# Pooled q and k summed on 128 partitions, dummy products between the first transposes, and a list schedule for a full TensorE clock

## The chip, the cores and the metric

The kernel runs on one core of one Trainium2 chip. The metric is device time in microseconds (us) for one execution. TensorE (PE) does the matrix products and transposes, VectorE (DVE) sums and elementwise work, ScalarE (ACT) activations and copies, GpSimd (POOL) some elementwise work, and SyncE (SP) issues the transfers.

## The reference

What is computed is an attention followed by two expert layers, all in float32. The attention is the sum of two parts: a local one, in which each position sees only positions less than 4 away, and a pooled one, in which q, k and v are averaged over groups of 4 positions (576 positions become 144), attended, and repeated 4 times.

```python
batch, n_heads, seq, head_dim = 4, 8, 576, 64        # q and k have a spread of 0.8, v of 0.1
q_d = q.reshape(B, H, Sd, factor, D).mean(axis=3)    # Sd = 144, factor = 4; k_d and v_d likewise
out_d = sm_attn(q_d, k_d, v_d)                       # softmax(q_d k_d^T / 8) v_d
out_up = np.repeat(out_d, factor, axis=2)
out_local = softmax(where(abs(i - j) < 4, q k^T / 8, -1e9)) v
x = (out_up + out_local) as 2304 tokens of 512
h = x @ w_in;   x = (s * max(h, 0)**2 + b) @ w_out   # 512 to 2048 and back
h = x @ w2_in;  out = (h - tanh(h)) @ w2_out
```

## The kernel before

Tokens are worked through in eight units of 288, two to a batch, for the first expert layer, and then in five blocks of 256 or 512 for the second. Each weight is split into a high and a low part, so that three products at the full rate of TensorE stand for one float32 product (`w_split`, `l1`, `l2_1`). A unit needs 16 steps; a step is 12 products `ph` into the hidden layer (L775), two activations and a split of the result on ScalarE and VectorE (`ph`, `gh`, `gl`), and, two steps later, 12 products `acc` (L808).

**Batch 0, at the start.** Its attention is done with dense products on TensorE: tokens of q and k are loaded (`tok`, SP, L511), transposed (`tokT`, L552, 36 transposes in 12 pieces), and copied to `KT` by VectorE (L560) and to `QT` by ScalarE (L556). Then come banded scores `S` (L582, L584), exponentials `bs` (L590), transposes `PT` (L597), and products with v, `O` (L607). The pooled part of this batch has the names `Sd`, `PdT` and `up`. `ORDER` lists these as words; `word` issues one. The word `k00` is a piece of k, `q00` of q. `warm` issues dummy products of the identity (L893) into a bank that nobody reads: 14 ahead of the words, and one ahead of each word that begins with e, f, p or u. Meanwhile the weights arrive in 32 pieces of 512 KB, and ScalarE and VectorE split them (`wraw`, `wf`, `w`; L707 to L761). SyncE's queue holds all these loads in one order.

**Batches 1 to 3.** The local attention of units 2 to 7 is on VectorE (`local_items`: products `pD`, sums `s`, weighted sums `O`), with shares for GpSimd (`pP`) and ScalarE (`pA`). At its end a unit's result `O` is transposed (`xt`, L305), the pooled part `upT` is added (`xq`, L323), and the sum is split (`xh` on ScalarE, `xl` on VectorE); the unit's first product L775 needs both. The pooled part is `down_items`, for each batch four rounds, one for each pair of heads (2m, 2m+1). A round loads q, k and v of both heads as two halves of 72 groups (L351, 72 partitions by two halves by two heads by 256 numbers). VectorE sums each four positions of q and of k (`pp`, L362, two sums a round), GpSimd those of v. Four transposes `qkps` (L384) bring q and k to 128 partitions, ScalarE copies them (`qkT`, L388, L389); then scores `S` (L400), exponentials `E`, `norm`, transposes `PT` (L436), and four products `up` (L451). The two heads of a round write `up` to partitions 0 to 63 and 64 to 127 of one bank, and one copy (L453) brings it to `upT`.

**What sets the order.** The body writes the instructions down step by step, with priorities; `list_schedule` then runs through time with the durations that `cost` gives, picks for each engine the ready instruction of best priority, and so fixes each engine's order. Engines keep that order at run time. `COLD` says until which time TensorE is taken to run at half speed: 55000 ns.

Of the kernel before, what the change touches and what calls it, by code (L numbers as in the profile page):

```python
# [29 lines left out]
G = S // 4  # L30
# [53 lines left out]
def attention_moe_moe_kernel(ctx: ExitStack, tc, q, k, v, w_in, w_out, s_in, b_in, w2_in, w2_out, out):  # L84
# [256 lines left out]
    def down_items(b):  # L341
# [3 lines left out]
        def load(hq):  # L345
            for nm, a in (("q", q), ("k", k), ("v", v)):
                base = (b * H + 2 * hq) * S * D
                t = raw_p.tile([128, 2, 2, 4, D], F32, tag="raw", name="raw72")
                for hf in range(2):
                    src = bass.AP(a.tensor, base + hf * GH * 4 * D, [[4 * D, GH], [S * D, 2], [1, 4 * D]])  # L350
                    sp.dma_start(out=t[:GH, hf].rearrange("p h r d -> p h (r d)"), in_=src)  # L351
                st[nm, hq] = t

        def padd(hq, nm):
            t = st[nm, hq]
            t2 = late.tile([GH, 2, 2, D], F32, tag="pp_" + nm, name="pp2")
            if nm == "v":
# [3 lines left out]
            else:  # L361
                dve.tensor_reduce(out=t2.rearrange("p a h d -> p (a h) d").unsqueeze(3),  # L362
                                  in_=t[:GH].rearrange("p a h r d -> p (a h) d r"), axis=AX, op=ALU.add)
            st[nm + "p", hq] = t2

        def loads(hq):
            def f():
                load(hq)
            return f

        def pools(hq):
            def f():
                for nm in "qkv":
                    padd(hq, nm)
            return f

        def qkt(hq):
            def f():
                if hq == 0:
                    upT[b] = late2.tile([128, 4, G], F32, tag="upT", name="upT")  # L380
                p_ = ps_sd.tile([128, 2, G], F32, tag="sd", name="qkps")
                for n, nm in enumerate("qk"):
                    for hf in range(2):
                        pe.transpose(p_[:, n, GH * hf:GH * hf + GH],  # L384
                                     st[nm + "p", hq][:, hf].rearrange("p h d -> p (h d)"), ident[:GH, :GH])
                t = late.tile([128, 2, G], F32, tag="qkT", name="qkT")

                act.activation(out=t[:, 0], in_=p_[:, 0], func=AF.Copy, scale=1.0 / 128.0)  # L388
                act.copy(out=t[:, 1], in_=p_[:, 1])  # L389
                st["T", hq] = t  # L390
            return f

        def scores(hq):
            def f():
                t = st["T", hq]
# [49 lines left out]
        def pvm(hq):  # L445
            def f():
                p_ = ps_sd.tile([128, G], F32, tag="sd", name="up")
# [8 lines left out]
        it.append((0, loads(0)))  # L456
        it.append((0, pools(0)))
        it.append((0, qkt(0)))
        for hq in range(4):
            if hq < 3:  # L460
                it.append((0, loads(hq + 1)))
            it.append((0.8, scores(hq)))
            it.append((0.8, norm(hq)))

            if hq < 3:
                it.append((0, pools(hq + 1)))
                it.append((0, qkt(hq + 1)))
            else:
                it.append((0, lambda: None))
            it.append((0, ptr(hq)))  # L470
            it.append((0, pvm(hq)))
# [815 lines left out]
COLD = 55000.0  # L1287
STORE_LAG = 8000.0

# [189 lines left out]
def list_schedule(ins, dep, soft, aps):  # L1479
# [22 lines left out]
    while wake:  # L1502
# [43 lines left out]
        while todo:  # L1546
# [10 lines left out]
            else:  # L1557
                go = end + ENG[eng[m]]
# [49 lines left out]
```

## Time and profile before

| | us |
|---|---|
| median of 3 runs | 946.79 (946.19 to 947.15) |
| the profiled execution | 947.49 |
| its span, first to last instruction | 945.7 |
| TensorE busy | 918.5 (97%) |
| VectorE busy | 730.3 (77%) |
| ScalarE busy | 504.1 (53%) |
| GpSimd busy | 155.0 (16%) |

The profiled execution is 0.7 us above the median, and 1.8 us of it lie outside the span. A busy share is a mean over stages that have different limits: what an edit is worth must be read in its own stage. Busy time of TensorE counts a product as long whether the clock is full or half, so the granted clock is read beside it.

### The profile page before, as it was taken

How to read it: one execution, taken by the hardware profiler on the slowest of the kernel's cores; microseconds unless marked ns; L12 is line 12 of the kernel's file. 1: busy time of each engine (PE TensorE's matmuls, PEld its weight loads, DVE VectorE, ACT ScalarE, POOL GpSimd, SP SyncE). 2: the span in 40 equal slices, each digit the busy share in tenths (PEclk: the TensorE clock that was granted, in tenths of full speed). 3: DMA queues.
4: the chain of work that ended last, by engine and by line, in shares of the span. 5: the costliest groups of instructions: out<-in, count | busy, mean ns of one | idle time of the engine just before them, and what ended most of it. 6: DMA issues, size and time to landing. Idle time of an engine off the chain costs nothing.

```text
span 945.7 us, 15470 instructions
## 1 busy us (share of the span) xinstructions
PE 918.5 (97%) x5690; PEld 822.7 (87%) x5690; DVE 730.3 (77%) x1156; ACT 504.1 (53%) x1270; POOL 155.0 (16%) x128
## 2 busy tenths in 40 slices
PE   7999999978999999998999999999999999999998
PEld 6888999868999999998999998888888888888886
DVE  4667899899899999997969767996768728676621
ACT  4679654534756557465668665663435415343321
POOL 1544343341411413133100000000000000000000
PEclk7559999997999999999999999999999999999999
DMA  9990042423214231231129978764443744442061
GB/s 227 319 340 36 27 159 63 144 86 99 88 61 137 68 118 39 65 95 43 48 68 397 345 279 275 258 212 155 132 136 112 254 146 140 151 135 88 30 193 45
DMA packets 82354, 137.39 MB, mean 145 GB/s; under 512 B 23414, under 2 KB 49254, under 8 KB 82278
## 3 DMA queue, kind: packets, MB, share of 16 engines
q1 hardware_dynamic: 80662, 134.04, 43.3%
q10 hardware_dynamic: 1616, 2.36, 0.9%
q8 instruction: 45, 0.74, 0.3%
q14 instruction: 31, 0.25, 0.1%
HBM read 111.66 MB, written 24.71 MB: 144 GB/s over the span
## 4 chain that ended last, share of the span: by engine, by line
PE 77%; DVE 10%; ACT 8%; issue 3%; SPq 1%; DMA 1%; DVEq 0%; ACTq 0%
PE acc L1039 20%; PE ph L775 18%; PE wb L1178 16%; PE acc L808 14%; ACT pA L254 2%; PE S L584 2%; DVE s L195 2%; DVE xq L323 1%; DVE pD L190 1%; PE O L607 1%; DVE O L266 1%; SPq L511 1%; ACT E L410 1%; PE warm L893 1%; DVE gl L796 1%
## 5 line engine op out<-in xcount | busy, mean ns | idle before, releaser
L775 PE MATMUL ph<-xh,w 128*128 128x288 f32 x1024 | 235.6, 304 | 2.5 <-DVE gl L796 1.7
L808 PE MATMUL acc<-gh,w 128*128 128x288 f32 (+1 forms) x1024 | 227.7, 298 | 1.5 <-DVE yst L831 0.9
L775 PEld LDWEIGHTS ph<-xh,w 128*128 128x128 f32 x1024 | 174.3, 192 | 8.7 <-DVE gl L796 3.7
L808 PEld LDWEIGHTS acc<-gh,w 128*128 128x128 f32 x1024 | 171.4, 189 | 3.0 <-issue 1.7
L775 PE MATMUL ph<-xl,w 128*128 128x288 f32 x512 | 154.5, 302 | 0.2 <-DVE xl L327 0.2
L808 PE MATMUL acc<-gl,w 128*128 128x288 f32 x512 | 151.4, 296 | 0.7 <-DVE gl L796 0.7
L1178 PE MATMUL wb<-xoh,w1r 128*128 128x512 f32 x448 | 147.4, 393 | 0.0
L1039 PE MATMUL acc<-w2r,gx 128*128 128x512 f32 x576 | 137.2, 390 | 0.0
L1039 PEld LDWEIGHTS acc<-w2r,gx 128*128 128x128 f32 x576 | 108.1, 188 | 23.3
L787 ACT ACTIVATE ph<-ph 128x288 f32<-128x288 f32 x128 | 50.8, 398 | 105.6 <-PE ph L775 101.8
L1178 PEld LDWEIGHTS wb<-xoh,w1r 128*128 128x128 f32 x448 | 83.9, 187 | 20.1 <-ACT w1r L1111 0.2
L775 PEld LDWEIGHTS ph<-xl,w 128*128 128x128 f32 x512 | 98.2, 192 | 1.4 <-issue 0.6
L808 PEld LDWEIGHTS acc<-gl,w 128*128 128x128 f32 x512 | 96.7, 189 | 1.5 <-DVE gl L796 0.9
L1178 PE MATMUL wb<-xol,w1r 128*128 128x512 f32 x224 | 88.2, 394 | 0.0
L796 DVE TENSOR_TENSOR gl<-ph,gh 128x288 fp32r<-128x288 f32 x128 | 57.8, 452 | 29.9 <-ACT gh L793 28.9
L254 ACT ACTIVATE pA<-V,a 128x64 f32<-128x64 f32 x198 | 54.0, 341 | 9.8 <-DVE a L243 6.1
L1172 DVE TENSOR_TENSOR u<-wb,u 128x512 f32<-128x512 f32 x64 | 43.9, 686 | 16.2 <-PE wb L1178 16.2
L793 ACT CAST gh<-ph 128x288 fp32r<-128x288 f32 x128 | 50.7, 398 | 6.4 <-PE acc L808 3.1
L1164 DVE TENSOR_TENSOR gx<-gT,gx 128x512 fp32r<-128x512 f32 x32 | 22.0, 689 | 39.0 <-ACT gx L1163 39.0
L788 ACT ACTIVATE ph<-ph 128x288 f32<-128x288 f32 x128 | 50.8, 398 | 2.4
L1178 PEld LDWEIGHTS wb<-xol,w1r 128*128 128x128 f32 x224 | 42.0, 187 | 9.6
L362 DVE TENSOR_REDUCE pp<-raw 72x256 f32<-72x1024 f32 x24 | 48.6, 2028 | 0.4 <-DMA raw<-in_q_dram 0.4
(167 smaller groups left out, 1573.1 us busy)
## 6 DMA issues: line engine op xcount, KB each, us to landing
w2r<-keep_b SPq DMA_DIRECT2D x48, 512.0 KB
wraw<-in_moe_w_in_dram SPq DMA_DIRECT2D x32, 512.0 KB
wraw<-in_moe_w_out_dram SPq DMA_DIRECT2D x32, 512.0 KB
w1f<-keep_a SPq DMA_DIRECT2D x32, 256.0 KB
w1f<-keep_s SPq DMA_DIRECT2D x32, 256.0 KB
keep_b<-w SPq DMA_DIRECT2D x12, 512.0 KB
y<-yst SPq DMA_DIRECT2D x36, 144.0 KB
K<-in_k_dram SPq DMA_DIRECT2D x5, 960.0 KB
```

What stands on the lines that cost most here:

```text
L254: act.activation(out=p_[:, t, h], in_=Vt[u][:, h, o + t], func=AF.Copy, scale=st["a"][:, h * TAU + t, o:o + 1])
L362: dve.tensor_reduce(out=t2.rearrange("p a h d -> p (a h) d").unsqueeze(3), in_=t[:GH].rearrange("p a h r d -> p (a h) d r"), axis=AX, op=A ...
L775: pe.matmul(p_, w_, x_, start=n == 0, stop=n == 3 * KC - 1)
L787: act.activation(out=p_, in_=p_, func=AF.Relu)
L788: act.activation(out=p_, in_=p_, func=AF.Square)
L793: act.copy(out=gh[:, :NB1], in_=p_)
L796: dve.tensor_tensor(out=gl, in0=p_, in1=gh[:, :NB1].bitcast(F32), op=ALU.subtract)
L808: pe.matmul(accs[u][e][:, :g_.shape[1]], w_, g_, start=i == first and n == 0, stop=i == last and n == 2)
L1039: pe.matmul(accs[j][t], g_, x_, start=i == 0 and n == 0, stop=i == NF - 1 and n == 2)
L1164: dve.tensor_tensor(out=t[:, 1], in0=g_, in1=t[:, 0].bitcast(F32), op=ALU.subtract)
L1172: add = lambda o, x, y: dve.tensor_tensor(out=o, in0=x, in1=y, op=ALU.add)
L1178: pe.matmul(b_, w1_op(q_, o, kc, i), xo[x][m][:, kc], start=n == 0, stop=n == 5)
```

## The change

It has three parts.

1. In `down_items`, q and k of a batch are no longer loaded by pairs of heads. The 4 x 144 = 576 groups of heads 0 to 3 are cut into rows of 128 (`ROWS`: 128, 128, 128, 128, 64); one tile holds such a row block of q and k, for heads m and m+4 side by side. One VectorE sum works on q and k together, so that a batch has 5 sums where it had 8 (15 for 24 in three batches), and 10 transposes where it had 16. All of a batch's pooled q and k stand in one tile `qkT` of 576 columns, and a round takes heads (m, m+4). The products `up` of a round write both heads to the same 64 partitions, side by side in columns; the copy to `upT` has 64 partitions by 288 columns where it had 128 by 144. The v part is as before, in functions of its own. The order of the items changes with it.
2. `word` issues three dummy products ahead of each of the 12 words k and q: 36 products.
3. In `list_schedule`, TensorE is taken to be at half speed until 6000 ns, where it was 55000, and an instruction of TensorE that depends on VectorE or ScalarE is taken to be ready 300 ns later (`SLACK`).

```diff
+        ROWS = [min(128, 4 * G - 128 * n) for n in range(5)]
+        def load(n):
+            def f():
+                t = raw_p.tile([128, 2, 2, 4, D], F32, tag="raw", name="rawqk")
+                for x, a in enumerate((q, k)):
+                    src = bass.AP(a.tensor, b * H * S * D + 128 * n * 4 * D, [[4 * D, ROWS[n]], [4 * S * D, 2], [1, 4 * D]])
+                    sp.dma_start(out=t[:ROWS[n], x].rearrange("p h r d -> p h (r d)"), in_=src)
...
-                dve.tensor_reduce(out=t2.rearrange("p a h d -> p (a h) d").unsqueeze(3),
-                                  in_=t[:GH].rearrange("p a h r d -> p (a h) d r"), axis=AX, op=ALU.add)
+        def pools(n):
+            def f():
+                r = ROWS[n]
+                t2 = late.tile([128, 2, 2, D], F32, tag="pp_qk", name="ppqk")
+                dve.tensor_reduce(out=t2[:r].rearrange("p a h d -> p (a h) d").unsqueeze(3),
+                                  in_=st["raw", n][:r].rearrange("p a h r d -> p (a h) d r"), axis=AX, op=ALU.add)
...
+                for x in range(2):
+                    pe.transpose(p_[:, x, :r], st["pp", n][:r, x].rearrange("p h d -> p (h d)"), ident[:r, :r])
+                t = st["T"][:, :, 128 * n:128 * n + r]
...
-                for kh in range(2):
-                    for h in range(2):
-                        pe.matmul(p_[64 * h:64 * h + 64, :], vp[:, kh, h, :], st["PT", hq][h][:, kh, :],
-                                  start=kh == 0, stop=kh == 1)
-                act.copy(out=upT[b][:, hq, :], in_=p_)
+                r = slice(64 * (hq % 2), 64 * (hq % 2) + 64)
+                for h in range(2):
+                    for kh in range(2):
+                        pe.matmul(p_[r, h], vp[:, kh, h, :], st["PT", hq][h][:, kh, :], start=kh == 0, stop=kh == 1)
+                act.copy(out=upT[b][r, hq // 2::2, :], in_=p_[r])
...
+        for f in (load(0), load(1), pools(0), qkt(0), load_v(0), pools(1), qkt(1), pool_v(0), load(2)):
+            it.append((0, f))
+        for m in range(4):
+            it.append((0, scores(m)))
...
+        if c in "kq":
+            warm(3)
...
-COLD = 55000.0
+COLD = 6000.0
+SLACK = 300.0
...
+                if eng[m] == "PE" and e in ("DVE", "Activation"):
+                    go += SLACK
```

The third part moves instructions on every engine. Three places follow; rows of the changed kernel have line numbers 3 to 5 higher.

The first is TensorE's queue at the start. Before, 14 dummies, the 36 transposes `tokT`, and then scores `S` one group at a time, with transposes `PT` after the second:

```order
L893 MATMUL warm<-ident 128x128 x14
L552 MATMUL tokT<-ident,tok 128x128 x36
L582 MATMUL S<-bandr,identr 96x408
L584 MATMUL S<-KT,QT 96x102 x4
L582 MATMUL S<-bandr,identr 96x408
L584 MATMUL S<-KT,QT 96x102 x4
L597 MATMUL PT<-ident,bs 102x96 x4
```

Now 17 dummies stand first, then four transposes and three dummies in turn, later three and three; the end of that row and the scores behind it are:

```order
L896 MATMUL warm<-ident 128x128 x3
L555 MATMUL tokT<-ident,tok 128x128 x2
L896 MATMUL warm<-ident 128x128 x3
L555 MATMUL tokT<-ident,tok 128x128 x2
L585 MATMUL S<-bandr,identr 96x408 x4
L587 MATMUL S<-KT,QT 96x102 x16
L585 MATMUL S<-bandr,identr 96x408
L587 MATMUL S<-KT,QT 96x102 x2
L600 MATMUL PT<-ident,bs 102x96
L587 MATMUL S<-KT,QT 96x102
```

Four score groups now stand in a row, and the first `PT` follows in the sixth group's place, one transpose at a time. ScalarE's queue up to the first activation of `ph` holds 27 passes over raw weights, 9 weight casts and 6 copies `bPT` before, and 24, 6 and 7 now.

The second place is TensorE where the first product of unit 2 needs its tokens. Before, all products of the units ahead of it are done, and then come the nine transposes `xt`:

```order
L808 MATMUL acc<-gl,w 128x288
L808 MATMUL acc<-gh,w 128x288
L305 MATMUL xt<-ident,O 128x128 x9
L384 MATMUL qkps<-ident,pp_2710 128x72 x2
L384 MATMUL qkps<-ident,pp_2712 128x72 x2
L400 MATMUL S<-qkT 72x144 x2
L775 MATMUL ph<-xh,w 128x288 x2
```

Now:

```order
L457 MATMUL up<-PTs,pp_2430 64x144 x4
L305 MATMUL xt<-ident,O 128x128 x4
L811 MATMUL acc<-gh,w 128x288
L811 MATMUL acc<-gl,w 128x288
L811 MATMUL acc<-gh,w 128x288
L778 MATMUL ph<-xh,w 128x288
L305 MATMUL xt<-ident,O 128x128 x4
L778 MATMUL ph<-xl,w 128x288
L778 MATMUL ph<-xh,w 128x288
L811 MATMUL acc<-gh,w 128x288
```

The transposes moved ahead of some 45 products of the units before; the ninth stands in the middle of them, and unit 2's own products follow after all of them.

The third is VectorE where the pooled part of batch 1 begins. Before:

```order
L823 COPY yst<-acc 128x288
L362 TENSOR_REDUCE pp_1740<-raw_1731 72x256
L362 TENSOR_REDUCE pp_1742<-raw_1734 72x256
L796 TENSOR_TENSOR gl<-ph,gh 128x288 x2
L195 TENSOR_REDUCE s<-pD 128x18
L407 TENSOR_REDUCE nm<-S 72x2 x2
L195 TENSOR_REDUCE s<-pP 128x18
```

Now:

```order
L826 COPY yst<-acc 128x288
L195 TENSOR_REDUCE s<-pD 128x18
L379 TENSOR_REDUCE ppqk<-rawqk 128x256
L799 TENSOR_TENSOR gl<-ph,gh 128x288 x2
L195 TENSOR_REDUCE s<-pP 128x18
L379 TENSOR_REDUCE ppqk<-rawqk 128x256
L799 TENSOR_TENSOR gl<-ph,gh 128x288
```

The first round's scores wait for two sums in both. From the start of VectorE's queue to its first `xq` of unit 2 there are 10 pooled sums before (8 of batch 1, 2 of batch 2) and 6 now (5 and 1), and one sum `s`, one `gl` and two additions `yst` fewer.

## Rows read from the trace of the kernel before

**Rows 1.** The page, part 1 and part 2: TensorE's busy time, granted clock in 40 slices.

```profile
PE 918.5 (97%) x5690; PEld 822.7 (87%) x5690; DVE 730.3 (77%) x1156; ACT 504.1 (53%) x1270; POOL 155.0 (16%) x128
PEclk7559999997999999999999999999999999999999
```

**Rows 2.** Stretches: start:end and length, busy us by engine, granted clock, DMA share, GB/s.

```profile
9.40:12.80 3.40, 1.44 (x9) 0.93 (x9) 1.73 (x3) 0.92 (x2) 0.00 (x0) 1.00 1.30 230
17.80:70.40 52.60, 52.60 (x266) 44.13 (x265) 33.86 (x82) 36.43 (x98) 22.38 (x23) 0.50 1.01 319
70.80:97.00 26.20, 25.98 (x205) 23.43 (x205) 18.98 (x45) 25.52 (x71) 11.94 (x9) 1.00 0.09 35
120.00:205.70 85.70, 84.78 (x641) 79.29 (x639) 77.86 (x111) 44.07 (x142) 33.33 (x33) 1.00 0.37 115
205.70:210.60 4.90, 0.00 (x0) 0.01 (x1) 4.90 (x7) 1.15 (x2) 0.88 (x2) 1.00 0.25 38
210.60:220.40 9.80, 6.70 (x26) 4.74 (x27) 9.80 (x19) 3.88 (x12) 5.61 (x2) 0.51 0.58 202
220.40:224.40 4.00, 4.00 (x18) 4.00 (x19) 3.73 (x3) 1.98 (x7) 1.27 (x1) 0.50 0.22 74
224.40:500.00 275.60, 269.88 (x2072) 261.67 (x2072) 250.35 (x363) 163.85 (x537) 67.67 (x34) 0.99 0.25 79
```

**Rows 3.** Timeline of TensorE at the start: start us, length us, what, records, idle before.

```profile
1.45 5.53 PE L893 MATMUL warm<-ident 128*128 128x128 f32 x28 [1.45 <-POOL ident L117]
6.82 1.91 PE L552 MATMUL tokT<-ident,tok 128*128 128x128 f32 x16
...
13.72 2.58 PE L552 MATMUL tokT<-ident,tok 128*128 128x128 f32 x11 [0.81 <-DMA tok<-in_q_dram]
```

**Rows 4.** Timeline of ScalarE, and its groups of lines from 14 to 70.4 us.

```profile
17.78 0.67 ACT L707 ACTIVATE wraw<-wraw 128x512 f32<-128x512 f32 x1 [0.34 <-DMA wraw<-in_moe_w_in_dram]
70.42 0.41 ACT L787 ACTIVATE ph<-ph 128x288 f32<-128x288 f32 x1
...
L707 ACT ACTIVATE wraw<-wraw 128x512 f32<-128x512 f32 x18 | 12.1, 677 | 1.1 <-DMA wraw<-in_moe_w_in_dram 1.1
L758 ACT CAST w<-wf 128x512 fp32r<-128x512 f32 x9 | 5.6, 624 | 0.8 <-DVE wf L753 0.8
```

**Rows 5.** SyncE's queue: the transfers of the weight pieces 13 to 16.

```profile
34.78 3.66 SPq L694 DMA_DIRECT2D wraw<-in_moe_w_out_dram  x4
```

**Rows 6.** VectorE: pooled sums (page, part 5), and other instructions in the timeline.

```profile
L362 DVE TENSOR_REDUCE pp<-raw 72x256 f32<-72x1024 f32 x24 | 48.6, 2028 | 0.4 <-DMA raw<-in_q_dram 0.4
...
17.20 1.15 DVE L570 TENSOR_REDUCE qd<-QT 128x72 f32<-128x288 f32 x3
33.27 0.45 DVE L627 TENSOR_REDUCE bnm<-Sd 72x2 f32<-72x288 f32 x1 [1.24 <-PE Sd L623]
...
199.73 0.46 DVE L796 TENSOR_TENSOR gl<-ph,gh 128x288 fp32r<-128x288 f32 x1 [0.23 <-ACT gh L793]
...
205.88 1.34 DVE L195 TENSOR_REDUCE s<-pD 128x18 f32<-128x1152 f32 x1
207.14 0.81 DVE L826 TENSOR_TENSOR yst<-acc,yst 128x288 f32<-128x288 f32 x2
```

**Rows 7.** TensorE: products `up` and `S` of the pooled part, two records to a product.

```profile
153.25 0.46 PE L451 MATMUL up<-PTs,pp 72*64 72x144 f32 x2
155.29 0.71 PE L400 MATMUL S<-qkT 64*72 64x144 f32 x4
440.44 0.71 PE L451 MATMUL up<-PTs,pp 72*64 72x144 f32 x8
```

**Rows 8.** The copies to `upT`: min/median/max ns, first and last start us.

```profile
L453 ACT COPY upT<-up x12: 268/278/280, 155.4 to 441.2; 128x144 f32<-128x144 f32 x12
```

**Rows 9.** Waits: who waited for whom, us in total, times, longest.

```profile
PE xt L305 <- DVE O L266: 4.9, 1, 4.9
DVE nm L407 <- PE S L400: 2.0, 5, 0.6
```

More of the change, by code (lines that the diff above doesn't have):

```diff
@@ L343, in down_items, with load_v, pool_v, f @@
         st = {}
-        def load(hq):
-            for nm, a in (("q", q), ("k", k), ("v", v)):
-                base = (b * H + 2 * hq) * S * D
+        ROWS = [min(128, 4 * G - 128 * n) for n in range(5)]
[5 more added lines that the diff above has]
+                    sp.dma_start(out=t[:ROWS[n], x].rearrange("p h r d -> p h (r d)"), in_=src)
+                st["raw", n] = t
+            return f
+        def load_v(m):
+            def f():
                 t = raw_p.tile([128, 2, 2, 4, D], F32, tag="raw", name="raw72")
                 for hf in range(2):
-                    src = bass.AP(a.tensor, base + hf * GH * 4 * D, [[4 * D, GH], [S * D, 2], [1, 4 * D]])
+                    src = bass.AP(v.tensor, (b * H + m) * S * D + hf * GH * 4 * D, [[4 * D, GH], [4 * S * D, 2], [1, 4 * D]])
                     sp.dma_start(out=t[:GH, hf].rearrange("p h r d -> p h (r d)"), in_=src)
[L352 to L357, printed above, removed]
+                st["v", m] = t
+            return f
+        def pool_v(m):
+            def f():
+                t = st["v", m]
+                t2 = late.tile([GH, 2, 2, D], F32, tag="pp_v", name="pp2")
                 t1 = t[:GH, :, :, 0:2, :]
@@ L369, in loads, with qkt @@
             return f
-        def pools(hq):
+        def qkt(n):
             def f():
[L373 to L379, printed above, removed]
-                    upT[b] = late2.tile([128, 4, G], F32, tag="upT", name="upT")
[L381 to L390, printed above, removed]
+                if n == 0:
+                    upT[b] = late2.tile([128, 4, G], F32, tag="upT", name="upT")
+                    st["T"] = late.tile([128, 2, 4 * G], F32, tag="qkT", name="qkT")
+                r = ROWS[n]
+                p_ = ps_sd.tile([128, 2, 128], F32, tag="sd", name="qkps")
+                for x in range(2):
+                    pe.transpose(p_[:, x, :r], st["pp", n][:r, x].rearrange("p h d -> p (h d)"), ident[:r, :r])
+                t = st["T"][:, :, 128 * n:128 * n + r]
+                act.activation(out=t[:, 0], in_=p_[:, 0, :r], func=AF.Copy, scale=1.0 / 128.0)
+                act.copy(out=t[:, 1], in_=p_[:, 1, :r])
@@ L394, in f @@
             def f():
-                t = st["T", hq]
+                t = st["T"][:, :, G * hq:G * hq + G]
                 ps = []
@@ L446, in f @@
             def f():
-                p_ = ps_sd.tile([128, G], F32, tag="sd", name="up")
+                p_ = ps_sd.tile([128, 2, G], F32, tag="sd", name="up")
                 vp = st["vp", hq]
-                for kh in range(2):
-                    for h in range(2):
-                        pe.matmul(p_[64 * h:64 * h + 64, :], vp[:, kh, h, :], st["PT", hq][h][:, kh, :],
-                                  start=kh == 0, stop=kh == 1)
-                act.copy(out=upT[b][:, hq, :], in_=p_)
-            return f
[L456 to L471, printed above, removed]
+                r = slice(64 * (hq % 2), 64 * (hq % 2) + 64)
[3 more added lines that the diff above has]
+                act.copy(out=upT[b][r, hq // 2::2, :], in_=p_[r])
+            return f
+        for f in (load(0), load(1), pools(0), qkt(0), load_v(0), pools(1), qkt(1), pool_v(0), load(2)):
+            it.append((0, f))
+        for m in range(4):
+            it.append((0, scores(m)))
+            if m < 3:
+                it.append((0, load_v(m + 1)))
+            it.append((0, norm(m)))
+            if m < 3:
+                for f in (pools(m + 2), qkt(m + 2), pool_v(m + 1)):
+                    it.append((0, f))
+            if m < 2:
+                it.append((0, load(m + 3)))
+            it.append((0, ptr(m)))
+            it.append((0, pvm(m)))
         return it
```

7 lines of the change are left out of this document (3 added, 4 removed).

## The prediction

> **What bounds the kernel now.** First the page: TensorE is busy 918.5 of 945.7 us, so nearly every microsecond saved must come out of TensorE's row. But busy time at half clock counts double, and the row of the granted clock shows two weak slices after the first, up to about 71 us [rows 1]. So next come the stretches, each with its clock [rows 2]. Three kinds can be told apart.
>
> From 17.8 to 70.4 us TensorE is busy without a gap at a granted clock of 0.50, that is at 1.2 GHz of 2.4. ScalarE is busy 36.4 of the same 52.6 us, VectorE 33.9: TensorE bounds this stretch, and only because its clock is low. From 70.8 to 97 us ScalarE is full (25.5 of 26.2), with TensorE full beside it. From 120 to 224 us VectorE works almost without rest (77.9 of 85.7, then 4.9 of 4.9, 9.8 of 9.8): TensorE runs out of work at 205.7, stands still for 4.9 us, is fed badly to 220.4, and has half clock from about 210.8 to 224.4. The waits name the cause: `xt` for VectorE's `O` [rows 9]. After that TensorE loses 5.7 us in 276 [rows 2].
>
> Why does the clock fall at the start? From 9.4 to 12.8 us TensorE ran only nine transposes, 1.4 us of work, while it waited for tokens, and it has half clock from then on [rows 2, 3].
>
> **The dummies.** The price of one: a transpose of the same shape takes 1.91/16 = 0.12 us at full clock [rows 3], a dummy is two such records, so 0.24 us; the 14 first dummies took 5.53 us, 0.40 each, mostly before the clock had risen, and half of that is 0.20. I take 0.22; 36 cost 7.9 us. Where TensorE waited for tokens (9.4 to 13.7) they cost nothing. In all, from 6.8 us: 3 dummies, 36 transposes at 0.12, 33 dummies at 0.22 end near 19.1, where the transposes ended at 16.3 before. So the scores start some 3 us later. In return the clock should not fall at 12.8, since TensorE then has no idle time there: half of its work is products like those that raised the clock at first.
>
> **The start at full clock.** TensorE's 52.6 us become 26.3, so ScalarE is the bound. Its queue up to the first activation of `ph` now holds 3 raw-weight passes and 3 casts fewer and one copy more: 3 x 0.68 + 3 x 0.62 - 0.48 = 3.4 us less [rows 4]. Its second piece still lands at 17.8 [rows 4], as the transfers keep their order. So 33.0 us of work from 17.8: no earlier than 50.8. It idled 16.2 us; its waits go round by VectorE and TensorE, and the later scores keep 3 us of them. I take half, 8.1 us: first activation at 58.9 where it was at 70.4 [rows 4], 11.5 us earlier. The 3.4 us that were put off are paid in the stretch where ScalarE is full, which leaves **-8 us**. Bounds: no idle at all, -16; the clock falls again, 0 (a rival). Transfers forbid nothing here: the first activation stands behind 16 weight pieces, and those are issued by 38.4 us [rows 5].
>
> **The pooled sums.** A sum of 72 partitions by 1024 numbers takes 2.03 us [rows 6]. The row of before has none of this kind on 128 partitions. If time went by all elements it would be 2.03 x 128/72 = 3.61, and 15 of them 54 us against 48.6; but a sum of 288 numbers takes 0.45 on 72 partitions and 1.15/3 = 0.38 on 128 [rows 6], so I take 2.03: 9 fewer save 18.3 us of VectorE. What that is worth depends on the place. Ahead of unit 2's first `xq` VectorE has 4 pooled sums fewer (8.1), one `s` (1.34), one `gl` (0.46) and two `yst` (0.81) [rows 6]: 10.7 us. TensorE's loss there is 18.7 us (205.7 to 224.4) less its work, 10.7 at half clock or 5.35 at full: 13.3 us. VectorE's 10.7 are less than that; the transposes now stand ahead of some 45 products, which cover the addition and the split behind them. I take **-10 us**. Bounds: the 4.9 us wait alone, and all 13.3.
>
> From 224 to 500 us TensorE loses 5.7 us idle, and a mean clock of 0.99 is 0.01 x 275.6 = 2.8 us of full clock [rows 2]: 8.5. The other sums saved help here, but VectorE is 91% busy and each late piece has its own chain. I take about a third, **-3 us**, between 0 and -8.5.
>
> **The products `up`.** Here the change costs. One product takes 0.46 us from issue to end; four of them in the two partition halves take 0.71. Two score products of the same 144 columns in one half take 0.71 already [rows 7]. So products in different halves of the array run side by side, and a further one in the same half adds 0.71 - 0.46 = 0.25. Now all four of a round write one half: 0.46 + 3 x 0.25 = 1.21, 0.50 more, 12 times: **+6 us** on TensorE; 0 if they fall where it waits.
>
> **What I cost at nothing.** 30 transposes for 48, of 128 rows for 72, are about equal (the same 3 us). ScalarE has 30 copies `qkT` for 24, 6 x 0.28 us if these cost as much as the copies to `upT` [rows 8], and the 12 copies to `upT` have twice the columns, at most 12 x 0.28 more: 5 us in all, in stretches where it is busy under 60% [rows 2]; if that cover went, the scores would come later by these. SyncE issues 54 loads a run for 72, and as many bytes. A sum needs its one buffer `ppqk` free, so VectorE can wait for TensorE's transposes of the block before; two buffers of one entry had the same rule before, and no such wait is in the rows.
>
> **Sum.** Against the profiled execution: 947.5 - 8 - 10 - 3 + 6 = 932.5 us. That run lay 0.7 above the median: 931.8, say **932**. With every term at its good end it would be 909, with every one at its bad end and the clock held 947.5 - 0 - 4.9 - 0 + 6 - 0.7 = 948.
>
> **The rivals.**
>
> *The clock holds through the first transposes and falls again among the scores.* For it: from 17.8 to 70.4 TensorE was without a gap and the clock still did not rise [rows 2], so this mix, products of 64 rows and transposes, is weak; at full speed it would also have gaps. Against it: from 120 to 205.7 TensorE had 0.9 us of idle time and full clock throughout [rows 2], so short gaps alone don't lower it. Then TensorE stays the bound, its work begins 3 us later, and the start gains nothing: 947.5 - 10 - 3 + 6 - 0.7 = 940. The Trainium skill has a rule for this, "TensorE: Matmul & The Clock Gate", section "Part 4: PE-mode transpose": a transpose does not count as work in the way that a product does when the clock is decided. The trace agrees as far as it goes: the fall at 12.8 followed a stretch of transposes alone. By that rule the many `PT` and `PdT` behind the scores would not hold the clock, and the time would be this rival's.
>
> *The dummies don't do what they are for.* The clock falls at 12.8 all the same. The 21 dummies then left cost 0.40 to 0.47 each, and everything is later by 9 us at a TensorE that is the bound: 947.5 + 9 - 10 - 3 + 6 - 0.7 = 949. Against it: the idle time that preceded the fall is filled.
>
> *Unit 2 waits for something else.* VectorE is done in time, but its `O` also needs shares from ScalarE and GpSimd, and `upT` needs four rounds; then only some 3 of the 10 us come: 939.
>
> *The order costs more than it gives (slower).* The 300 ns make the schedule put TensorE's transposes and scores behind products of the steps, while VectorE or ScalarE waits for them. There are 75 such crossings in the pooled rounds (25 a batch) and 18 sets `xt`, 93 in all; with VectorE 91% busy a wait of it is not repaid. From 15/93 = 0.16 us more at each the change loses; at 0.25 us it is +23, 955. Against it: VectorE waited only 2.0 us in five times for `S` [rows 9].
>
> **How the numbers follow.** Forecast 0.53, clock falls later 0.20, unit 2 held by another 0.10, dummies fail 0.07, order 0.10. Leaving out the last two and a thin tail below, the range is 915 to 945. Faster by over 0.2% (less than that can't be told from no change) 0.83, within 0.2% 0.05, slower 0.12.
>
> **What would show it.** In the profile after: a granted clock of 1.00 from 12.8 to beyond 20 us; first activation of `ph` near 59; 15 sums at 2.0 us; no wait of 4.9 us for `O`, and clock 1.00 at the start of unit 2; four `up` at about 1.2 us. I am wrong if the sums grow with partitions, if the clock reads 0.50 in the score stretch, or if TensorE's idle time between 224 and 600 us grows.

## The result, and the profile after

The changed kernel takes **930.62 us** (median of 4 runs, 929.73 to 934.84) beside 946.72 for the kernel before in the same series: a ratio of 0.9834, with a 95% interval from 0.9812 to 0.9855, so 16 us faster. The profiled execution has a span of 929.0 us, where it was 945.7.

The page's part 1 and its row of the granted clock, in 40 slices, to be read beside [rows 1]:

```profile
PE 909.0 (98%) x5744; PEld 814.6 (88%) x5744; DVE 705.8 (76%) x1147; ACT 506.0 (54%) x1276; POOL 151.9 (16%) x128
PEclk9869999999999999999999999999999999999999
```

TensorE is busy 9.5 us less although it runs 36 dummies more (and 18 transposes fewer; two records to each). The stretches of the changed kernel (start:end and length, busy us of PE, PEld, DVE, ACT and POOL with their counts, granted clock, DMA share, GB/s) answer to [rows 2]:

```profile
12.80:40.40 27.60, 27.26 (x245) 23.30 (x243) 18.75 (x52) 20.39 (x64) 9.06 (x9) 1.00 1.06 276
40.40:61.00 20.60, 17.22 (x93) 14.20 (x93) 15.16 (x36) 16.84 (x39) 7.67 (x9) 0.50 0.97 309
17.80:60.05 42.25, 38.54 (x285) 31.56 (x285) 29.58 (x81) 33.09 (x94) 16.37 (x17) 0.77 1.02 285
70.80:97.00 26.20, 26.20 (x215) 24.07 (x216) 17.73 (x46) 25.46 (x72) 9.14 (x7) 1.00 0.14 57
186.70:198.40 11.70, 10.90 (x83) 9.93 (x81) 11.70 (x22) 5.26 (x14) 4.46 (x2) 1.00 0.42 134
198.40:224.00 25.60, 24.64 (x180) 23.25 (x180) 25.20 (x36) 16.36 (x52) 8.28 (x3) 1.00 0.48 150
224.00:500.00 276.00, 271.10 (x2031) 261.16 (x2032) 238.42 (x373) 170.44 (x539) 69.63 (x32) 1.00 0.29 96
```

The clock is full from 12.8 to 40.4 us, falls to half until about 61, and is full to the end. The row from 17.80 ends at the first activation of `ph`; it will be read against the prediction's sum for the start. Unit 2 starts at 198.4 us without the idle 4.9 us before it and at a full clock. The new sums (VectorE's groups of lines, by form: busy us and mean ns) and a round of `up` (TensorE's timeline: start, length) answer to [rows 6] and [rows 7]:

```profile
L379 DVE TENSOR_REDUCE ppqk<-rawqk 128x256 f32<-128x1024 f32 x12 | 23.9, 1992 | 0.4 <-DMA rawqk<-in_k_dram 0.3
L379 DVE TENSOR_REDUCE ppqk<-rawqk 64x256 f32<-64x1024 f32 x3 | 5.9, 1983 | 0.0
```

```profile
146.81 1.19 PE L457 MATMUL up<-PTs,pp 72*64 72x144 f32 x8
```

A sum costs 1.99 us on 128 partitions where 72 took 2.03. A round of `up` takes 1.19 us where it took 0.71.

Where the time came from is read best from milestones in the traces: when ScalarE begins the first activation of `ph`, and when TensorE begins the first `ph` product of a step (16 steps to a unit; unit 2 begins with step 32). In us:

| kernel | median | first activation | step 31 | step 33 | step 64 | step 127 |
|---|---|---|---|---|---|---|
| before | 946.7 | 70.4 | 195.2 | 222.7 | 334.2 | 557.1 |
| after | 930.6 | 60.1 | 186.7 | 200.5 | 319.3 | 540.1 |
| gain | 16.1 | 10.4 | 8.5 | 22.2 | 14.9 | 17.1 |

So the start gives 8.5 us, the passage into unit 2 another 13.8, and some 5 go again behind it. In size that is nearly the sum that was predicted. The experiments show that the first of these does not need the added dummies, and that the second comes only in part from the sums.

Such a gain depends on where it is read, because the new order also moves work. At step 8 the changed kernel is 13.8 us ahead (89.0 for 102.8), at step 12 only 8.9 (115.7 for 124.7): part of the attention of batch 0 is put off to steps 8 to 12 (18 records of `S` there where there were 9, 40 of `O` where there were 32). From step 12 on the lead of the start hardly changes until step 31. In the passage from step 31 to 33 TensorE ran 8 records of `S` and 6 of `qkps` before, and runs none and 2 now, so a little of the 13.8 us is work left for later.

### The profile page after: what moved, and what is told of

Same layout as the page of the kernel before. It is cut to its first block, busy times and chain, and to the rows that moved or that the text cites. A ratio compares the mean times of both kernels' runs of the same rounds, so it can differ in the third digit from the quotient of the medians.

```text
span 929.0 us, 15495 instructions
## 1 busy us (share of the span) xinstructions
PE 909.0 (98%) x5744; PEld 814.6 (88%) x5744; DVE 705.8 (76%) x1147; ACT 506.0 (54%) x1276; POOL 151.9 (16%) x128
## 4 chain that ended last, share of the span: by engine, by line
PE 79%; DVE 12%; ACT 4%; issue 2%; DMA 2%; SPq 1%; POOL 0%; DVEq 0%; POOLq 0%; ACTq 0%
PE acc L1044 20%; PE ph L778 18%; PE wb L1183 17%; PE acc L811 15%; PE warm L896 2%; PE up L457 1%; DVE pD L190 1%; PE S L587 1%; DVE s L195 1%; DVE xq L323 1%; PE S L405 1%; DMA rawqk<-in_k_dram 1%; PE O L610 1%; DVE ppqk L379 1%; DVE gl L799 1%
## 5 line engine op out<-in xcount | busy, mean ns | idle before, releaser
L1183 PEld LDWEIGHTS wb<-xoh,w1r 128*128 128x128 f32 x448 | 83.9, 187 | 20.5 <-DVE gl L1035 0.6
L258 POOL TENSOR_TENSOR pP<-V,a 128x1152 f32<-128x1152 f32 x12 | 33.6, 2804 | 123.2 <-DVE a L243 51.9
```

What stands on the lines that cost most here:

```text
L258: eng.tensor_tensor(out=p_, in0=Vt[u][:, :, o:o + TAU, :].rearrange("p h t d -> p t h d"), in1=aw.to_broadcast([128, TAU, 2, D]), op=ALU.mult)
L1183: pe.matmul(b_, w1_op(q_, o, kc, i), xo[x][m][:, kc], start=n == 0, stop=n == 5)
```

## The experiments

My theory was that the added dummies give the start (through the clock), that the fewer sums give unit 2, and that `up` costs 6 us. The rival was that the schedule's new figures (`COLD`, `SLACK`) give either.

### The three parts, alone and in pairs

**The sums alone** (the new `down_items` in the kernel before):

```diff
-                it.append((0, pools(hq + 1)))
-                it.append((0, qkt(hq + 1)))
...
+        for f in (load(0), load(1), pools(0), qkt(0), load_v(0), pools(1), qkt(1), pool_v(0), load(2)):
+            it.append((0, f))
```

> The kernel before with the new pooled half alone (15 sums on up to 128 partitions, `up` in one half of the partitions); no dummy products, the old clock and slack figures in the schedule. My theory (fewer VectorE sums give unit 2 its gain): the first relu of `ph` stays at 70.4 us, the first `ph` product of unit 2 comes about 10 us earlier than before (217.2), the wait of 4.9 us for `O` and the fall of the clock at 210.8 us are gone; with +5.8 us for the serial `up` products (12 rounds x 0.48) and about -3 in the rest, 940 us (937 to 943). Rival (unit 2's gain comes from the new schedule): unit 2 starts near 217 as before, and the time is 946 to 952, since only the price of `up` is left.

Measured: 950.4 us (940.0 to 953.5), ratio 1.002 (0.9994 to 1.0045). One of the ten runs took 940.0, the figure of the theory; the others took 948.5 or more, as the rival had it, and the profile is of one of these. The first activation stays at 69.0, and the way from step 31 to step 33 takes 19.9 us where it took 27.5, so the sums do speed up the passage, by 7.7. But the median isn't 940: what was gained goes again behind step 33.

**Everything but the sums** (the old `down_items` in the changed kernel):

```diff
-        for f in (load(0), load(1), pools(0), qkt(0), load_v(0), pools(1), qkt(1), pool_v(0), load(2)):
-            it.append((0, f))
...
+                it.append((0, pools(hq + 1)))
+                it.append((0, qkt(hq + 1)))
```

> The changed kernel with the old pooled half (24 sums on 72 partitions, `up` in both halves); dummies and the new figures of the schedule stay. My theory: the first relu stays near 60 us, unit 2 gains no more than the start does (first product near 208.5, against 217.2 before and 198.4 after); the time is about 938 us (936 to 940). Rival (the schedule gives unit 2 its gain, the sums nothing): unit 2 starts at 198 to 200, and without the serial `up` products the time is 924 to 930.

Measured: 947.3 us, ratio 0.9995 (0.9984 to 1.0007): no gain at all, against 938 from one theory and 924 to 930 from the other. The start is kept (first activation 61.5), the passage takes 20.5 us, and all of it is lost again by step 64.

**The added dummies taken away:**

```diff
-        if c in "kq":
-            warm(3)
```

> The changed kernel without the 36 dummy products among the token transposes; the rest stays, the schedule made for a full clock too. My theory (the dummies hold the clock): granted clock 0.50 from 12.8 us on as before, first relu near 70 us, time about 939 us (937 to 942). Rival (the schedule's order gives the start its gain): the first relu at 58 to 62 us and the time 929 to 932 us.

Measured: **932.1 us**, ratio 0.9823 (0.9797 to 0.985), first activation at 58.9. The rival is right. The 36 dummies are worth nothing that these runs can tell: the two intervals overlap almost wholly. Nor are they needed to keep the clock up at 12.8 us, where it fell before; here it is full until about 33 us without them:

```profile
12.80:33.00 20.20, 19.07 (x172) 15.81 (x170) 15.26 (x41) 16.75 (x56) 4.69 (x4) 1.00 1.06 217
```

**The added dummies alone** (in the kernel before):

```diff
+        if c in "kq":
+            warm(3)
```

> The kernel before with the 36 dummy products alone; old pooled half, old figures of the schedule. My theory (the clock alone gives the start): clock 1.00 from 12.8 us to about 40 us, first relu at 59 to 62 us, time 938 to 940 us. Rival (the schedule must be made for the full clock, or the order keeps the gain back): first relu at 65 us or later, time 943 to 947 us.

Measured: 971.7 us, ratio 1.0252 (1.0224 to 1.028), first activation at 86.4. Both figures were wrong: this is 24 us slower. The rival had the direction (the order keeps the gain back), not the size. ScalarE's timeline in this run (start, length, what, and in brackets its idle time and what ended it) shows where the start is held up:

```profile
15.33 0.70 ACT L707 ACTIVATE wraw<-wraw 128x512 f32<-128x512 f32 x1 [4.30 <-DMA wraw<-in_moe_w_in_dram]
...
21.45 0.68 ACT L707 ACTIVATE wraw<-wraw 128x512 f32<-128x512 f32 x1 [1.43 <-DMA wraw<-in_moe_w_in_dram]
22.02 0.87 ACT L556 ACTIVATE QT<-tokT 128x384 f32<-128x384 f32 x1
...
30.40 0.68 ACT L707 ACTIVATE wraw<-wraw 128x512 f32<-128x512 f32 x1 [3.85 <-DMA wraw<-in_moe_w_out_dram]
30.97 0.62 ACT L556 ACTIVATE QT<-tokT 128x256 f32<-128x256 f32 x1
```

And TensorE's waits from 18 to 33 us (us in all, times, longest), with its stretch there:

```profile
PE S L584 <- ACT QT L556: 10.0, 2, 6.0
PE S L582 <- DVE KT L560: 1.6, 1, 1.6
```

```profile
18.20:32.00 13.80, 2.13 (x11) 1.36 (x9) 8.04 (x15) 6.75 (x11) 7.05 (x7) 0.64 1.03 252
```

With TensorE taken to be slow for 55 us, the schedule believes that the transposes and their 36 dummies end late, and puts passes over weight pieces ahead of the last evictions `QT` in ScalarE's queue. At run time the transposes end at 18.5, but the queue stands and waits for the transfer of a piece, with `QT` behind it: TensorE works 2.1 of 13.8 us.

**The schedule's figures alone** (in the kernel before):

```diff
-COLD = 55000.0
+COLD = 6000.0
+SLACK = 300.0
...
+                if eng[m] == "PE" and e in ("DVE", "Activation"):
+                    go += SLACK
```

> The kernel before with the two figures of the schedule alone (PE counted as slow for 6 us instead of 55; 300 ns more from a product to VectorE or ScalarE); no added dummies, old pooled half. My theory, changed after the first four runs (the schedule made for a full clock gives the start, the added dummies almost nothing on top; the sums are needed for what follows): first relu of `ph` at 59 to 62 us, granted clock 1.00 beyond 20 us, falls of the clock again between 200 and 330 us, time 944 to 949 us. Rival (with the old sums the added dummies are needed): clock 0.50 from about 13 us, first relu at 68 us or later, time 950 us or more.

Measured: 946.2 us, ratio 0.9985 (0.9972 to 0.9999), first activation at 59.6. The theory formed after the first four runs held: the schedule alone brings the first activation as early as the whole change does, the clock falls again (at 207, 269 and 317 us), and without the new sums the gain is lost. Of a lead of 10.9 us at the first activation 6.8 are left at step 12, where the changed kernel has 8.9, and 3.7 at step 31, where it has 8.5. (The expectation names the direction of the 300 ns the wrong way round: it is TensorE's instruction that is taken to be ready later.)

**Dummies and sums, the old figures:**

```diff
-COLD = 6000.0
+COLD = 55000.0
...
-SLACK = 300.0
+SLACK = 0.0
```

> The changed kernel with both figures of the schedule as before; dummies and new sums stay. My theory (dummies without the schedule hold ScalarE's evictions of `QT` back behind weight pieces, whatever the sums): TensorE idle for over 5 us on `QT` between 19 and 33 us, first relu at 75 us or later, time 955 to 975 us. Rival (what the dummies alone did is chance of one order, and the sums undo it): first relu at 58 to 64 us, time 930 to 943 us.

Measured: 962.6 us, ratio 1.0173 (1.0155 to 1.0191), first activation at 87.0, TensorE waiting 9.6 us for `QT`. As the theory said.

The eight combinations, medians in us (those of before differ by up to 0.9 between series), with the way from step 31 to 33:

| dummies | figures | sums | median | first activation | step 31 to 33 |
|---|---|---|---|---|---|
| | | | 946.7 | 70.4 | 27.5 |
| yes | | | 971.7 | 86.4 | 18.7 |
| | yes | | 946.2 | 59.6 | 20.6 |
| | | yes | 950.4 | 69.0 | 19.9 |
| yes | yes | | 947.3 | 61.5 | 20.5 |
| | yes | yes | 932.1 | 58.9 | 13.7 |
| yes | | yes | 962.6 | 87.0 | 22.7 |
| yes | yes | yes | 930.6 | 60.1 | 13.8 |

No part alone gains more than 0.2%. The schedule and the sums gain 15 to 16 us together, and the dummies need the schedule not to harm. (Where the start is some 16 us late, the passage from step 31 to 33 is short for another reason too: VectorE has had that time for its work.)

### The two figures apart

```diff
-COLD = 6000.0
+COLD = 55000.0
```

> The changed kernel with the slow stretch of the schedule back at 55 us; the 300 ns of slack, dummies and sums stay. My theory (the length of the slow stretch makes the start, the slack what follows): first relu at 70 us or later, yet no fall of the clock between 200 and 600 us; time 940 to 962 us. Rival (the slack makes the start): first relu at 58 to 62 us, time 929 to 934 us.

Measured: 968.0 us, ratio 1.0215 (1.0177 to 1.0252), first activation at 87.5. The start is lost as expected; but the clock did fall again, at 188, 229 and 362 us, so the 300 ns by themselves don't prevent that.

```diff
-SLACK = 300.0
+SLACK = 0.0
```

> The changed kernel with the 300 ns of slack taken away; the slow stretch of 6 us, dummies and sums stay. My theory (the slack keeps TensorE from short waits in units 2 to 6, and so the clock up): first relu at 58 to 62 us, but two or three falls of the clock between 200 and 600 us, time 936 to 946 us. Rival (the slack does nothing): no fall after the start, time 929 to 933 us.

Measured: 955.2 us (947.2 to 962.5), ratio 1.0069 (1.0039 to 1.01), first activation at 74.7. Two falls of the clock between 200 and 600 us came, as the theory had it (at 381 and 419 us), but the start was lost too, which neither side expected. The ten runs spread widely: three took 947 to 950 us, the others 954.8 or more, and the profile is of one of 959.4. TensorE's timeline has one wait for `QT`, and its stretch behind it is at half clock though it is busy throughout:

```profile
20.14 0.59 PE L587 MATMUL S<-KT,QT 64*96 64x102 f32 x6 [0.97 <-ACT QT L559]
```

```profile
23.00:44.00 21.00, 21.00 (x91) 16.57 (x90) 6.26 (x14) 9.46 (x39) 7.21 (x7) 0.52 0.99 303
```

### Does the wait for `QT` make the bad start?

In two kernels the schedule alone was told that the first pieces land later, so that it would put `QT` first. Here in the kernel with dummies and sums and the old figures:

```diff
             end = dma + 900.0
+            if end < 45000.0 and "moe_w" in str(getattr(aps[n][0][0].bass_ap.tensor, "name", "")):
+                end = max(end, min(end + PIECES, 26000.0))
...
+PIECES = 8000.0
```

> The run without the schedule's new figures (dummies and new sums, 962.6 us), where the schedule alone is told that the first weight pieces land up to 8 us later than it assumed (no later than 26 us), so that it queues ScalarE's six evictions of `QT` ahead of them; no data moves otherwise. My theory (the lost start is ScalarE waiting for the DMA of a piece with evictions queued behind it, and TensorE idle for 10 us): no wait of TensorE for `QT` over 1.5 us, clock 1.00 at 22.4 us, first relu at 58 to 65 us instead of 87, time 933 to 945 us. Rival (the lost start is the order made for a slow TensorE itself): first relu at 75 us or later, time 952 us or more.

Measured: 958.4 us, ratio 1.0118 (1.0089 to 1.0146), first activation at 83.4. The edit did half of what it should: four of six evictions went ahead, and the two largest waits in the first 90 us are now these:

```profile
PE PT L600 <- ACT bs L593: 4.5, 4, 1.8
PE S L587 <- ACT QT L559: 3.2, 2, 2.0
```

The wait for `QT` fell from 9.6 to 3.2 us and the start came 3.6 us earlier, with another 4.5 us of waits for `bs` in its place and half clock from 21.4 us. The numbers are the rival's, but as the edit left a wait, the test is inconclusive: it shows that the wait for `QT` is not all.

The same in the kernel without the slack:

> The run without the slack (955.2 us; one wait of 1.0 us of TensorE for `QT` at 19.2 us, clock 0.50 from 22.7 us, first relu at 74.7 us), with the schedule told the same of the first weight pieces. My theory (that one wait let the clock fall, and the half clock cost the rest): no wait for `QT`, clock 1.00 from 6 to 35 us at least, first relu at 57 to 63 us, time 930 to 944 us. Rival (the slack is needed for the order of scores and transposes itself): clock 0.50 by 27 us, first relu at 70 us or later, time 948 us or more.

Measured: 949.2 us, ratio 1.0022 (0.9998 to 1.0046), first activation at 69.1 (74.7 without the edit), nearer to the rival than to the theory. The wait for `QT` is gone and TensorE had no idle time at all from 12 to 40 us, yet its clock fell at 26.2. Its stretches, and rows of its timeline ahead of the fall:

```profile
12.00:26.20 14.20, 14.20 (x117) 12.07 (x116) 9.01 (x16) 6.75 (x19) 1.98 (x2) 1.00 1.08 255
26.20:40.00 13.80, 13.80 (x59) 10.48 (x58) 4.26 (x9) 6.18 (x25) 5.96 (x6) 0.51 0.92 304
```

```profile
22.88 0.41 PE L587 MATMUL S<-KT,QT 64*96 64x102 f32 x2
23.22 0.29 PE L600 MATMUL PT<-ident,bs 96*102 96x96 f32 x1
23.44 0.41 PE L587 MATMUL S<-KT,QT 64*96 64x102 f32 x2
23.79 0.29 PE L600 MATMUL PT<-ident,bs 96*102 96x96 f32 x1
```

So the clock fell without a wait: from 18.6 to 26.0 us TensorE ran score products and transposes with no dummy among them. That pointed to the dummies that the kernel had before, 16 of them ahead of words of the scores, and to where each schedule puts them. TensorE's time in dummies (product `warm`), by stretch, first before and then without the added dummies:

```profile
19.00:31.00 12.00, 0.00 (x0) 0.00 (x0) 0.50 1.05 248
31.00:45.00 14.00, 5.34 (x16) 4.07 (x17) 0.50 1.02 368
45.00:66.00 21.00, 5.32 (x16) 4.02 (x16) 0.50 0.98 310
```

```profile
7.00:19.00 12.00, 1.90 (x13) 1.85 (x14) 1.00 1.16 246
19.00:31.00 12.00, 3.43 (x20) 2.88 (x20) 1.00 1.09 199
31.00:45.00 14.00, 0.00 (x0) 0.00 (x0) 0.58 0.96 301
```

Before, all 16 (32 records) stand between 31 and 66 us, at half clock, and take 10.7 us. The schedule made for a full clock puts all of them before 31 us, some of them where TensorE would wait for tokens.

### Without any dummy among the scores

```diff
-WARM = 1
+WARM = 0
```

(in the kernel without the added dummies)

> The run without the 36 added dummies (932.1 us) also without the 16 older ones that the kernel before had among its scores; the 14 ahead of the transposes, the schedule's new figures and the new sums stay. My theory, from where the dummies stand in the runs so far (the schedule made for a full clock moves the 16 older ones from 31 us and later to 9.9 to 25 us, and there they hold the clock): granted clock 0.50 from 12 to 20 us on, first relu at 67 to 78 us, time 940 to 952 us. Rival (the order of scores and transposes under the new figures holds the clock, or the gain needs none): first relu at 57 to 62 us, time 929 to 934 us.

Measured: 938.8 us, ratio 0.9907 (0.9889 to 0.9925). Each theory has half: the clock does fall, at 20.8 us, yet the first activation stands at 59.6 all the same. So the first activation comes early without a full clock beyond 20.8 us. TensorE's stretches up to the first `ph` product, of this kernel and then of the kernel before:

```profile
12.80:20.80 8.00, 7.92 (x67) 5.93 (x66) 7.54 (x16) 6.05 (x18) 0.00 (x0) 1.00 1.04 284
20.80:55.90 35.10, 31.14 (x171) 24.11 (x169) 22.30 (x59) 25.67 (x75) 15.20 (x15) 0.50 1.00 267
```

```profile
12.80:20.80 8.00, 6.80 (x31) 5.54 (x29) 4.81 (x10) 5.66 (x11) 0.00 (x0) 0.50 1.07 291
20.80:64.90 44.10, 44.10 (x233) 37.42 (x232) 27.64 (x68) 30.06 (x83) 20.37 (x22) 0.50 1.01 312
```

The first `ph` product comes 9.0 us earlier, and the two traces give an account of it, which is not a test. Before, the 44.1 us from 20.8 held 10.7 us of dummies and 33.4 of work, without a gap. Here they hold 31.1 us of work (more was done by 20.8, at full clock) and 4.0 of idle time: 10.7 + 2.3 - 4.0 = 9.0. In this account the older dummies are the largest term, in the stretch that they were to help.

That this run is 6.7 us slower than the one with the 16 older dummies comes mostly from one place behind the start: by step 8 it is 6.4 us behind, 5.2 of them lost from step 4 on. There TensorE waits 5.5 us for `gh`, with half clock from 79 to 86 us, and ahead of that ScalarE stands 3.2 us before a weight cast:

```profile
ACT w L761 <- DVE wf L756: 3.2, 1, 3.2
```

```profile
76.00:86.00 10.00, 4.54 (x25) 4.26 (x23) 5.48 (x15) 8.69 (x24) 2.51 (x2) 0.66 0.02 6
```

With this, and with the work put off to steps 8 to 12, nothing of the early start is left: step 12 begins at 124.3 us, for 124.7 before, and the 8.6 us that this kernel gains come from the passage into unit 2. The run shows that the first activation doesn't need the full clock; it doesn't show that a lead won that way lasts.

### The price of `up`

Each round pairs heads of opposite parity, so that its results lie in both halves of the partitions again:

```diff
-                    src = bass.AP(v.tensor, (b * H + m) * S * D + hf * GH * 4 * D, [[4 * D, GH], [4 * S * D, 2], [1, 4 * D]])
+                    src = bass.AP(v.tensor, (b * H + m) * S * D + hf * GH * 4 * D, [[4 * D, GH], [(4 + (m ^ 1) - m) * S * D, 2], [1, 4 * D]])
...
-                r = slice(64 * (hq % 2), 64 * (hq % 2) + 64)
+                r = [slice(64 * ((hq ^ h) % 2), 64 * ((hq ^ h) % 2) + 64) for h in range(2)]
...
-                act.copy(out=upT[b][r, hq // 2::2, :], in_=p_[r])
+                for h in range(2):
+                    act.copy(out=upT[b][r[h], hq // 2 + 2 * h, :], in_=p_[r[h]])
```

> The changed kernel, with each round pairing heads of opposite parity, so that its two `up` results lie in both halves of the partitions again (two copies of upT a round instead of one; the first scores wait for three sums instead of two). My theory (the products of one half run one after another and cost 0.48 us a round on TensorE, 12 rounds): `up` x8 in 0.71 us instead of 1.19, no new fall of the clock, time 924 to 928 us. Rival (TensorE's idle time hides it, or another order opens new waits): `up` x8 in 0.71 us, but the time 929 to 936 us.

Measured: 936.1 us, ratio 0.9901 (0.9875 to 0.9926), 5.5 us slower than the changed kernel. A round of `up` is back at its old length:

```profile
154.37 0.71 PE L457 MATMUL up<-PTs,pp 72*64 72x144 f32 x8
```

In all 12 rounds TensorE spends 10.5 us in `up` before, 15.8 in the changed kernel and 12.2 here, so the price is real. From step 33 to step 127 this kernel takes 333.0 us where the changed one takes 339.6. Only 8 of the 12 rounds lie there, worth 8 x 0.48 = 3.8 us, so the 6.6 us less are not the price of `up` alone; TensorE's idle time from 224 to 500 us is also shorter, 2.5 us for 4.9. Against this the other order of the sums costs 7.6 us up to step 33 (208.1 instead of 200.5, with a wait of 2.2 us behind `xq` and half clock from 203 to 210 us), and a wait of 2.4 us at 580 us lets the clock fall in the tail. The theory had no new fall of the clock. The rival's second half, that another order opens new waits, is what happened: this way of saving the price costs as much elsewhere.

### Why the sums are needed

With the schedule's figures, with and without the new sums, TensorE's waits from 205 to 330 us and its three worst stretches differ as follows. The figures alone:

```profile
PE PT L436 <- DVE E L424: 3.6, 2, 2.0
PE PT L436 <- DVE xq L323: 1.9, 1, 1.9
PE ph L775 <- ACT xh L326: 1.6, 1, 1.6
```

```profile
205.00:235.00 30.00, 27.18 (x188) 26.08 (x188) 28.09 (x45) 14.76 (x43) 4.68 (x3) 0.89 0.37 116
262.00:280.00 18.00, 16.04 (x106) 14.41 (x105) 17.83 (x29) 8.24 (x25) 4.69 (x3) 0.81 0.33 116
310.00:330.00 20.00, 16.36 (x91) 14.55 (x89) 12.66 (x14) 7.21 (x23) 6.24 (x4) 0.74 0.25 79
```

The figures and the sums, without the added dummies:

```profile
PE ph L778 <- DVE xl L327: 1.3, 1, 1.3
PE ph L778 <- DVE gl L799: 0.8, 1, 0.8
```

```profile
205.00:235.00 30.00, 29.91 (x226) 29.27 (x226) 29.02 (x41) 18.30 (x60) 4.83 (x4) 1.00 0.32 108
262.00:280.00 18.00, 18.00 (x130) 16.42 (x129) 15.45 (x24) 12.09 (x41) 6.43 (x3) 1.00 0.43 140
310.00:330.00 20.00, 19.17 (x145) 18.70 (x144) 18.24 (x27) 9.13 (x25) 2.33 (x2) 1.00 0.15 42
```

With 24 sums VectorE brings `E` and `xq` late, TensorE waits about 2 us at a time, and at each of these places the clock falls to half for a while: 8.4 us idle in the three stretches, and 30 x 0.11 + 18 x 0.19 + 20 x 0.26 = 11.9 us of full clock lost, beside 0.9 and 0 (the two overlap, since the clock also counts while TensorE waits). From step 31 to step 64 the gap between the two kernels grows from 3.5 to 18.1 us. Here a late piece of VectorE costs TensorE its wait and then the clock. The two kernels differ by the first part of the change as a whole (sums, transposes, pairs of heads, order of the items); that it is the number of sums is read from these waits, and no run changed it alone.

## Why the prediction was right, point by point

The time was right (932 predicted, 930.6 measured, range 915 to 945), in part by luck: the start came out in size by another way than forecast, unit 2 gave 3.8 us more and what follows took 2.5 us more. Of its terms:

- **Start, -8: right in size (-8.5), wrong in cause.** The step that failed is "TensorE's 52.6 us become 26.3, so ScalarE is the bound": the clock was to be the lever, and the added dummies were to pull it. From 17.8 us to the first activation TensorE was busy 38.5 of 42.3 us, at a mean clock of 0.77, and not 26.3. The clock did stay full from 12.8 to 40.4, as the sign asked, and the first activation came at 60.1 for 58.9. But without the 36 dummies it comes at 58.9 and the clock stays full to 33; with no dummy among the scores and half clock from 20.8 it comes at 59.6. The prediction read "busy without a gap" in [rows 2] as needed work, and did not ask what the work was: 10.7 of those 52.6 us were the kernel's own older dummies, and the schedule's new figures moved them out of the way. The two figures, which the prediction gave no price of their own, bring the first activation forward. Its sum for ScalarE came out, 33.1 us of work and 9.2 of idle time (33.0 and 8.1 predicted). What stays open: the kernel before with its 16 dummies taken out and nothing else was not run, so the 10.7 us are read from the trace and from one run that differs in the order as well, ScalarE's order with it. Open too is what part the full clock has in keeping the lead, as the run without it lost its lead by step 12.
- **Price and place of the dummies: right.** In the changed kernel three dummies and two transposes repeat every 0.89 us, and the last transpose ends at 19.1 (predicted 19.1). They were simply not needed.
- **Unit 2, -10: 13.8 measured, about half from the sums.** The passage from step 31 to 33 is 7.7 us shorter with the sums alone, 6.9 with the schedule alone, 13.8 with both; read from step 12 on it is 6.1, 3.9 and 13.3. The sum that was worked out, 10.7 us less of VectorE, is not what TensorE got from them; the schedule's part was missing.
- **Rest, -3 and `up`, +6: together +3 predicted, +5.5 measured** from step 33 to the end. The price of `up` was right, a round at 1.19 us for 0.71 and 5.35 us more of TensorE in all 12 rounds, though 4 of these lie ahead of step 33. The -3 shows in [rows 2] against the same stretch now: from 224 to 500 us 4.9 us idle at 1.00, for 5.7 at 0.99, which is 0.8 + 2.8 = 3.6 us. So these terms do not make +5.5. Units 2 and 3 (step 33 to 64) lose 7.3 us; the work left for later by the passage is part of it, and the remainder stays open. The sums' worth in this stretch appears when the schedule is the new one in both, and is then some 8 us (126.5 us from step 33 to 64 with old sums, 118.8 with new).
- **Sums on 128 partitions at 2.03 us: right** (1.99).
- **Rival "the clock falls again among the scores": its event came, its price did not.** The clock fell at 40.4, and scores ran at 0.50 behind it, which the prediction had named as a sign of being wrong. By its working the start would then gain nothing; it gained 8.5. These runs don't settle whether transposes are to blame. Ahead of the fall at 40.4 TensorE ran mostly products `O`, `Sd` and `up`, with 1 us of transposes in the last 7:

```profile
35.63 1.57 PE L610 MATMUL O<-vw,bPT 102*96 102x65 f32 x16
37.14 1.01 PE L646 MATMUL PdT<-ident,bE 72*72 72x72 f32 x8
```

  In the run without any dummy among the scores TensorE ran transposes alone from 7.4 to 13.1 us, with 1.6 us of work from 9.4 to 12.8, and kept the full clock to 20.8; before, it ran them alone from 6.8, with 1.4 us of work in the same stretch, and the clock fell at 12.8. So the sparse stretch that the prediction blamed for the fall doesn't bring it every time. The rule on transposes that the prediction cites from the Trainium skill ("TensorE: Matmul & The Clock Gate", section "Part 4: PE-mode transpose") is neither borne out nor refuted by this.
- **Rival "the order costs more than it gives": not for this change.** The added dummies under the old figures do cost that much (+24 and +16 us beside before), but there is no slack in those kernels, so this isn't the rival's mechanism at TensorE's 93 crossings. What their traces show is ScalarE's queue at `QT`, a wait of 10.0 and 9.6 us; what part of the loss it makes stays open, since the run that took two thirds of it away gained 4 us.

## What to carry to other kernels

A list schedule is only as good as the speed it assumes: with dummies added while it still took TensorE for slow, the kernel was 24 us slower, and correcting the assumption moved filler work off the critical stretch. Before crediting a gain to a clock, list what the busy time consists of; fillers placed at half clock on a full engine take its time. Parts of a change can be worth nothing alone and 15 us together, so test the pairs, and take out the part that looks like the cause. Follow a gain to a later milestone too: one kernel's early start was gone by step 12.

## What the runs showed of the hardware

- TensorE can be busy without any idle time and still lose its full clock: 14.2 of 14.2 us busy up to 26.2 us, then half, in the run with late pieces and no slack. What it ran from 18.6 to 26.0 us were score products and transposes.
- The sum over four positions takes as long on 64, 72 and 128 partitions (1.98, 2.03 and 1.99 us).
- VectorE's passes over weight pieces, 0.42 us (`wraw`) and 0.68 (`wf`) as a rule, took up to 1.8 us in a few places of each run (at most 9 of 112), and in each of these GpSimd was at work beside them; others beside GpSimd (5 to 21 a run) took their usual time. In the run without any dummy among the scores two such places fill the 3.2 us for which ScalarE waited for `wf`:

```profile
72.00 1.51 DVE L712 TENSOR_SCALAR wraw<-wraw 128x512 int32<-128x512 int32 x1
73.43 1.77 DVE L756 SCALAR_TENSOR_TENSOR wf<-wraw 128x512 int32<-128x512 int32 x1
```
